# A gated mix of two long convolutions: masked sines on ScalarE, gate sums with the input as the stationary operand, another layout of the gathered kernel, mixing by group

## The chip, the cores and the metric

The kernel runs on one core of a Trainium2 chip. Its engines work side by side, each through its own queue in order: PE (TensorE: matmuls, and the loads of their stationary operands, shown as PEld), DVE (VectorE), ACT (ScalarE), POOL (GpSimd) and SP, which here only issues DMAs. The metric is the device time of one execution in microseconds; lower is better.

## The reference

Inputs are bf16; the sequence has 2048 steps and 448 lanes. From `u` three things are computed and mixed:

```python
g = sigmoid((u * gate_w).sum(-1, keepdims=True))
# a: K[d,l] = Re sum_n C*dt*B * exp(dt*A*l)   (448 lanes, 256 modes, 2048 steps)
a = causal_conv(u, K) + u * Dskip             # by zero-padded FFTs of 4096
# b: kv = (4-tap shift of k) * v
b = u * (causal_conv(kv, ssm_k) + kv * ssm_D)
return g * a + (1 - g) * b
```

## The kernel before

**Layout.** The 128 partitions hold 4 groups of lanes times 32 blocks of time: partition 32 g + a, and on the free axis 64 steps of time and 112 lanes (`uu`, `kt`, `vt`, `ug` are all [128, 64, 112]). The loops go over `H` = 0 to 3, a window of 28 lanes of each group, so 112 lanes at once.

**A convolution** is a transform, a product and an inverse, all by matmuls with matrices of sines that the kernel makes itself. `spread` takes one lane's [128, 64] slice as stationary operand and `Wc` as moving operand, into `zs` (32 frequencies k, 4 groups x 28 lanes). `transform` multiplies each k by `s2_W`. `swapped` makes a copy `zsS` with the real and imaginary halves exchanged, by two DMAs; `products` multiplies `zs` and `zsS` with the other factor. `stage_a` with `R` (`sa_R`) gives `U`, and `stage_b` with `G` (`sb_G`, 64 x 2 matrices of 128 x 128) gives back the time axis. `G` is masked: the columns of group g are non-zero only in the rows of that group. Every matmul stage goes through PSUM (three buffers with the tag "ps"), and is evacuated by ACT (`evac`), or by ACT and DVE in turn (`evac_two`, whose argument i chooses).

**Constants** are made at the start. `stage_b` in the class `Consts` writes phases with DVE, takes their sine with ACT (`sb_v`), and multiplies it with the four columns of the mask on DVE, 16 products in all.

**The kernel K** of convolution a is made by `KGen` in eight blocks of 14 lanes per group. DVE builds powers in `TQ` and `TP` (tiles kg_TQ, kg_TP, with kg_P between), PE sums over modes into `pk`, ACT evacuates to `kg_S`, `gather` arranges the steps by small matmuls into two PSUM tiles that are evacuated to `KT`, and `spread` with `WcK` takes it on. `Tables` makes the exponentials and sines of each pair of blocks in `ET`.

**The gate.** DVE multiplies `uu` with the weights into `ug`, 14 matmuls with a matrix of ones (128 x 128, 512 moving columns) sum eight lanes at a time, DVE reduces, ACT takes a tanh, and DVE makes `gt`, `gb` = g and `og` = 1 - g.

**The end.** Window 3 of convolution a is done in two halves of 14 lanes (`transform_half`, `last`, `stage_a_half`). `mix` multiplies `ug` (result of b) with og, `uu` (by then result of a for windows 0 to 2) with gb, and adds the two for 84 lanes, in eight instructions by halves of the time axis. The last `stage_b` gives four banks of 16 steps; for each DVE multiplies with the gate (`ept`), adds into `ug`, and four DMAs store it, two from SP's queue and two from ACT's.

**Order.** Nothing is issued as the program text runs. `Order` records all 6437 calls, and `issue` replays them in the order of the list `ORDER`, which is written out; each engine keeps that order. The one line that does it is 146, so the profile shows L146 for everything, and groups are told apart by their tiles:

```python
for f, args, kw in self.calls[int(a):int(b or a) + 1]:
    ins = f(*args, **kw)
```

Of the kernel before, what the change touches and what calls it, by code (L numbers as in the profile page):

```python
# [17 lines left out]
P = 128  # L18
# [4 lines left out]
NQG = 4  # L23
# [18 lines left out]
    "681 106 18 113 40 1 270 145 0 114 39 257 274 272 268 275 253 105 109 269 273 255 271 276 256 254 240 104 149 266 "  # L42
    "277 241 267 24 251 3 242 632 672 625 103 108 50 252 634 22 614 244 258 31 38 112 9 604 623 259 111 64 94 42 679 "
    "110 261 10 633 260 46 41 19 278 624 122 61 674 635 49 153 147 30 281 98 282 4 263 246 120 95 2 13 84 45 121 247 "
    "11 154 99 14 155 76 280 16 626 151 47 97 77 96 156 680 21 607 117 20 262 636 25 248 56 608 7 63 15 128 264 17 75 "
    "32 72 37 627 146 55 48 639 23 44 88 150 66 637 29 90 78 249 69 640 118 8 152 83 36 80 629 85 53 107 57 43 628 "
    "101 51 12 119 631 87 62 65 59 630 58 116 74 100 159 35 638 60 52 115 92 265 70 605 79 180 91 6 124 33 27 67 5 26 "
    "71 123 54 82 28 68 102 148 89 659 86 81 125 93 606 34 73 660 144 670 616 667 671 243 668 673 609 245 132 665 661 "
    "250 126 666 662 279 669 663 283 675 129 676 611 677 610 130 157 160 127 181-188 158 131 133-134 170 136 143 135 "
    "220 142 171-178 189 141 161-168 179 200 190 201-208 169 210 304-311 209 294-301 312-320 617 321 230 191-198 "  # L50
    "211-218 199 302-303 615 331-338 219 678 322-329 613 346 339 221-228 612 229 364-379 664 618 231-238 380 330 239 "
    "347-362 621-622 284-291 363 619 381-396 293 397-405 292 1093 620 406 341 1094 434-441 340 1091 416-423 442 1092 "
    "407-414 342 424 343 415 344-345 551 657 561 565 595 658 566 592 560 553 591 443 554-555 550 547 446 466-481 552 "
    "549 548 444 449-464 482 573 769-784 586 465 569 587 500-507 445 508 786-801 785 557 425-432 581 683 641 483-498 "
    "684 642 802 568 596 687 597 572 578 689 582 686 583 598 433 584 688 499 685 1095 562 577 509-516 556 588 563 "
    "690-703 558 589 567 559 590 1109 2471 564 579 593 580 570 594 447 574 571 599 575 527-534 448 643 704 518-525 "
    "137 2516 600 2517 138 601 2477 139 2478 603 602 576 140 1097 1096 2475 2493 535 1098 2494 1099 526 536-543 1105 "
    "705 1100 2472 706 544 1101 644 708 2480 1103 2476 585 707 1106 517 1108 2473 545 653 2474 645 2479 656 646 649 "
    "1111 647 682 651 1107 650 726-741 1113 648 1110 654 1102 655 760-767 652 742-758 1112 1835 768 1114 709-724 546 "
    "759 803-818 725 1115 819 898-905 1104 829-844 906 1117 1120 889-896 845 820-827 1834 828 1122 880-887 897 1836 "  # L60
    "907-914 1837 888 1116 934-941 915 863-878 1838 942 1118 1498-1505 1840 1506 1447-1462 879 952-959 1119 1842 960 "
    "916-923 1124 1463 846-861 1121 1123 924-932 862 1839 1443 1464-1479 933 943-950 1125 1444 1841 2495 1541-1556 "
    "1843-1844 1126 951 1480 2485 1127-1350 2486 1845-1846 2487 2496-2498 1445 2499 2502 2500 1446 2501 1507-1522 "
    "1351-1368 1848 1558-1565 1847 2503 1369 1850 2504 1370-1409 1849 2505 1410 2507 1851 1411-1418 2506 1853 2508 "
    "1852 1419 2482 2509 1566 1420-1427 2481 1523 1854 1618-1625 2483 1855 1524-1539 1856 2518 1428 2484 2491 1626 "
    "2490 1429-1434 1857 1540 1861 961-1024 2510 1859 2512 1557 1858 1481-1496 2492 1672-1679 1863 1830 1435 2520 "
    "1680 1829 1860 1436-1441 1832 1025 1442 1601-1616 1497 1831 1862 2236-2243 1617 1636-1643 2511 2521 2513 1864 "
    "1026-1089 2522 2543 2514 2526 2525 1865-2088 2488 2528 2527 2489 1090 2530 2533 2544 2556 2244 2545 1833 2546 "
    "2515 2547 2519 1644 2548 2529 2523 2531 2549 2524 2550 2539 1663-1670 2538 2089 2559 1645-1652 2558 2542 2554 "
    "1671 3315 2552 2090-2106 2537 1681-1688 1653 2555 1567-1582 2561 1689 2557 2932-2947 1583 2563 1627-1634 2560 "  # L70
    "2569 1635 1654-1661 2107 1584-1599 2562 1662 2571 2564 2108-2147 2535 2182 1600 2565 2181 2148 1699-1762 2566 "
    "2536 2567 2532 2534 2551 2541 2948 2174-2179 2568 2949-2964 1763 2180 1690-1697 2540 2149-2156 2965 3951 2573 "
    "1764-1827 1698 2553 2157 2570 2184 2167-2173 2158-2165 3958 3996 2166 2183 3959 3954-3955 3957 3960 3953 3965 "
    "3956 2245-2260 3314 3952 1828 2572 2296-2303 2261 2279-2294 3966 2574 2304 2202-2217 3997 2295 3316 2185-2200 "
    "2575 2218-2234 3323 2576-2799 3317 2201 3318 2235 3319 3967 3321 3324 3326 3974 3968 2323-2330 3973 2800 3329 "
    "3975 2894-2901 3327 3331 2331 3976 3333 2801-2817 2921-2928 2902 3962 2332-2339 3325 3961 2929 3335 2903-2910 "
    "3328 3337 3963 3330 3682-3697 2911 3964 3977 3332 2818 2305-2312 3978 3338 2340 2819-2858 2313 2912-2919 "
    "3339-3340 2859 3320 2314-2321 2920 2869-2876 3334 2322 2992-3007 3979 3322 2893 2262-2277 3998 3987 3980 3969 "
    "3971 2892 3986 3981 3970 3336 3988 3999 2278 3989 3341 3972 2341-2404 3008 4005 3983 3982 3698 3342 3984 4006 "
    "3343 4022 2931 2983-2990 2966-2981 4020-4021 4019 2991 3344 2982 4008 3345-3568 4001 4014 2930 4009-4010 4016 "  # L80
    "4012 4023 4017 4011 4007 4000 2877 4795 3991-3992 4002 2405 3985 4025 3990 4794 4003 3130-3137 3993 4027 4796 "
    "4004 4026 3139-3146 3994 3569 4797 3995 3043-3050 4036 3138 4798 2878-2883 4039 4038 4028 3051 3716-3723 2884 "
    "4041 2406-2469 3724 4029 3147 4043 4030 4013 3699-3714 2470 3103-3110 2885-2890 4032 3715 3009-3024 4034 3025 "
    "4799 3121-3129 3086-3101 4035 4801 3111-3119 4024 4037 4463-4470 3102 4804 4803 3120 3026-3041 4040 2891 3661 "
    "3052-3067 4806 3042 4042 4045 2860-2867 3662 4018 3069-3084 3068 4031 2868 3166-3173 4471 4047 3588-3627 3085 "
    "4033 3148-3155 4053 3628 3665-3680 4015 3156 3570-3586 4044 5371 4052 3681 3157-3164 4046 3165 3175-3182 4054 "
    "3587 4809 3249-3312 3183 4049 3174 4811 4051 5374 5372 3663 5378-5379 5377 5376 3654-3659 3184-3247 5375 3313 "
# [534 lines left out]
def body(  # L622
# [188 lines left out]
    def block(j):  # L811
# [3 lines left out]
        if KA[H] is None:  # L815
            KA[H] = qt([P, 32, 4 * NC], "zsK")
# [158 lines left out]
```

## Time and profile before

| what | us |
|---|---|
| three runs | 310.83, 310.70, 307.97 (median 310.7) |
| the profiled execution | 308.75 |
| its span, first to last instruction | 307.0 |
| busy in the span: DVE, ACT, PE | 275.5, 250.3, 220.9 |
| table loads on ACT | 15 of 1.28 each |
| mean granted clock of PE | 0.859 of full |

In a line of groups, out<-in are tiles, then come partitions x elements and types, the count, busy time and mean nanoseconds of one instruction, and behind the second bar the idle time in front of them with what ended it. In the answer by stretches the columns are the stretch, its length, busy time (and instructions) of PE, PEld, DVE, ACT and POOL, the granted clock of PE, the share of the DMA engines and GB/s. Lines of the timeline have start, duration, engine, operation and tiles.

### The profile page before, as it was taken

The page shows a single profiled execution, that of the slowest core. Times are in us where ns is not written, and L with a number is a line of the kernel's source. Part 1 is how long each engine was busy: PE and PEld are TensorE (multiplying, and loading weights), DVE is VectorE, ACT ScalarE, POOL GpSimd, SP SyncE. Part 2 cuts the span into 40 slices and gives each one's busy share as a digit, 9 for nine tenths or more (in the row PEclk, how much of TensorE's full clock was granted, in tenths as well). Part 3 has the DMA queues.
Part 4 walks back from the last instruction along what each step waited for, and adds up shares of the span by engine and source line. Part 5 has one row for each costly group of instructions (what it writes and reads, how often), then busy time and mean ns, then how long its engine had stood idle before and what let it go on. Part 6 is the DMA issues. An engine that isn't in the chain of part 4 may idle for free.

```text
span 307.0 us, 11924 instructions
## 1 busy us (share of the span) xinstructions
PE 220.9 (72%) x5287; PEld 192.6 (63%) x5287; DVE 275.5 (90%) x549; ACT 250.3 (82%) x404; POOL 19.1 (6%) x122
## 2 busy tenths in 40 slices
PE   0049973581787688796986598988868989789750
PEld 0013553441777588686976598877867979679740
DVE  8999999969999999999899999798999899972771
ACT  4743589999999499996899999999998997858610
POOL 9101102700000000000000000000000000000000
PEclk9995997768598679997998579979867799999975
DMA  5899999137005003060005002400031000550066
GB/s 110 170 194 167 164 170 253 55 67 113 2 2 122 4 15 49 5 165 4 4 4 121 4 2 46 127 0 6 2 84 42 2 2 4 122 125 5 2 113 129
DMA packets 53380, 21.33 MB, mean 69 GB/s; under 512 B 48720, under 2 KB 51664, under 8 KB 53328
## 3 DMA queue, kind: packets, MB, share of 16 engines
q1 hardware_dynamic: 48768, 19.42, 34.2%
q10 hardware_dynamic: 4560, 1.15, 1.9%
q8 instruction: 41, 0.67, 0.9%
q14 instruction: 11, 0.09, 0.1%
HBM read 10.01 MB, written 3.21 MB: 43 GB/s over the span
## 4 chain that ended last, share of the span: by engine, by line
ACT 39%; PE 26%; DVE 25%; issue 4%; DMA 4%; SPq 0%; DVEq 0%; ACTq 0%
ACT zs L146 14%; ACT ET L146 9%; PE ps_c L146 7%; ACT zsK L146 5%; PE ps_a L146 5%; PE pk L146 5%; ACT U L146 4%; DMA zsS<-zs 4%; PE ps_b L146 3%; PE ps_v L146 3%; PE ps L146 3%; DVE zs L146 2%; DVE zsS L146 2%; DVE kg_P L146 2%; DVE kg_TP L146 2%
## 5 line engine op out<-in xcount | busy, mean ns | idle before, releaser
L146 ACT CAST zs<-ps_c 128x1024 bf16<-128x1024 f32 (+1 forms) x48 | 43.2, 928 | 2.3 <-PE ps_c L146 2.1
L146 DVE TENSOR_TENSOR kg_P<-kg_TQ,ET 128x896 bf16<-128x896 bf16 (+2 forms) x64 | 44.1, 708 | 0.3
L146 ACT CAST zs<-ps 128x896 bf16<-128x896 f32 x48 | 43.5, 930 | 0.8 <-PE ps L146 0.7
L146 PEld LDWEIGHTS <-s_W 128*128 128x128 bf16 x544 | 30.4, 103 | 15.1 <-issue 11.5
L146 PE MATMUL ps_a<-sa_R,zs 128*128 128x128 bf16 x224 | 35.6, 247 | 1.9 <-ACT zs L146 1.3
L146 PE MATMUL pk<-kg_TP,kg_TQ 128*21 128x32 bf16 x1792 | 29.6, 238 | 9.5 <-issue 5.6
L146 PE MATMUL ps_a<-sa_R,zsS 128*128 128x128 bf16 x224 | 34.9, 244 | 1.6 <-DVE zsS L146 1.6
L146 PE MATMUL ps<-zs,s_W 128*128 128x112 bf16 x384 | 28.1, 223 | 9.7 <-ACT zs L146 8.0
L146 PEld LDWEIGHTS <-kg_TQ 128*21 128x21 bf16 x1792 | 27.5, 121 | 11.2 <-issue 10.5
L146 ACT CAST U<-ps_a 128x1024 bf16<-128x1024 f32 (+2 forms) x32 | 30.2, 955 | 3.5 <-PE ps_a L146 3.3
L146 PEld LDWEIGHTS <-zsS 128*128 128x128 bf16 x224 | 31.0, 154 | 3.3 <-DVE zsS L146 1.7
L146 PE MATMUL ps_b<-U,sb_G 128*128 128x28 bf16 x1024 | 28.3, 177 | 5.2 <-ACT U L146 4.9
L146 PEld LDWEIGHTS <-zs 128*128 128x128 bf16 x224 | 30.8, 153 | 1.9 <-DVE zs L146 0.6
L146 PEld LDWEIGHTS <-sb_G 128*128 128x128 bf16 x1024 | 27.5, 97 | 6.4 <-issue 5.6
L146 DVE TENSOR_TENSOR kg_P<-kg_TP,ET 128x1792 bf16<-128x1792 bf16 (+1 forms) x32 | 30.9, 970 | 0.1
L146 DVE TENSOR_TENSOR kg_TQ<-kg_P 128x896 bf16<-128x896 bf16 (+2 forms) x64 | 27.7, 445 | 0.1
L146 PEld LDWEIGHTS <-scratch 128*128 128x128 bf16 x65 | 7.4, 115 | 30.1 <-issue 27.0
L146 PE MATMUL ps_c<-WcK,kg_KT 128*64 128x128 bf16 x224 | 19.0, 294 | 7.9 <-ACT zsK L146 6.6
L146 ACT CAST zsK<-ps_c 128x512 bf16<-128x512 f32 (+2 forms) x28 | 21.6, 780 | 3.2 <-PE ps_c L146 2.9
L146 ACT ACTIVATE ET<-ks_ph 128x448 bf16<-128x448 int16 x40 | 22.7, 599 | 1.2 <-DVE ks_ph L146 1.2
L146 ACT ACT_TABLE_LOAD x15 | 19.2, 1283 | 4.1 <-DMA kt<-in_B_k_dram 3.9
L146 PEld LDWEIGHTS <-kg_KT 128*64 128x64 bf16 x224 | 16.5, 209 | 9.2 <-issue 6.7
(127 smaller groups left out, 468.5 us busy)
## 6 DMA issues: line engine op xcount, KB each, us to landing
zsS<-zs SPq DMA_DIRECT2D x16, 448.0 KB, 5.1
kt<-in_B_k_dram SPq DMA_DIRECT2D x16, 112.0 KB, 3.1
uu<-in_A_u_dram SPq DMA_DIRECT2D x4, 448.0 KB, 8.5
skraw<-in_B_ssm_k_dram SPq DMA_DIRECT2D x16, 112.0 KB, 4.5
vt<-in_B_v_dram SPq DMA_DIRECT2D x4, 448.0 KB, 8.9
xfd<-ks_hold SPq DMA_DIRECT2D x2, 672.0 KB, 4.9
ks_xf<-xfd SPq DMA_DIRECT2D x3, 336.0 KB, 3.3
out_dram<-ug SPq DMA_DIRECT2D x8, 112.0 KB, 3.6
```

The lines of the kernel that those rows point to most:

```text
L146: ins = f(*args, **kw)
```

## The change

Five things, and a new list.

1. The mask of `G` holds the scale of the phase instead of 1/2048, and ACT writes `G` directly: four sines for each of the four quarters, with the mask's column as per-partition scale (outside the group the scale is 0, and so is the sine). The sixteen products and `sb_v` go. The factor 1/2048 is put on `R`, by one DVE instruction.
2. The gate's sums: `gwt` holds the weights, masked by block of time; 112 matmuls take a lane of `uu` (64 columns) as stationary operand and 32 columns of `gwt` as moving operand. The result, 64 x 32, is copied four times side by side, transposed with an fp32 identity, and goes to the tanh. The seven products with DVE and the reduce go.
3. `KT` is [128, 14, 64] for [128, 64, 14]: a lane's 64 columns lie side by side.
4. `mix` goes by window: eleven instructions of 28 lanes. Window 3's product with uu, og and the windows 0 and 1 can stand early; window 2's product with gb and add wait for its result.
5. In block 7 the second evacuation of `gather` and of `spread`, and in `stage_a_half` the second of each half, go to DVE.

The new list holds 6531 calls. It orders all engines' instructions and the DMAs anew, not those of the changed parts alone. Two places matter for what follows: at the start, the sixteen sines stand on ACT among the evacuations of `ps_v` to `kt`, with all of the products that make `kvt` behind each other on DVE; in the tail, PE has both parts of window 2's `stage_b` ahead of the last `stage_a_half`, and DVE has window 2's two mixing instructions ahead of the first `ept`, and the four stores follow each other.

```diff
@@ stage_a (constants)
         nc.scalar.activation(R[:], low16(ph.rearrange("p i b -> p (i b)")), ACT.Sin, scale=PHASE)
+        nc.vector.tensor_scalar(out=R[:], in0=R[:], scalar1=1.0 / 2048, scalar2=None, op0=ALU.mult)
@@ stage_b (constants)
-            v = pool.tile([P, 16, 2, 32], bf16, name="sb_v", tag="kg_P4", bufs=2)
-            nc.scalar.activation(v[:].rearrange("p b r a -> p (b r a)"), low16(ph[:].rearrange("p b r a -> p (b r a)")),
-                                      ACT.Sin, scale=PHASE)
             for g in range(4):
-                nc.vector.tensor_scalar(out=G[:, b0:b0 + 16, :, g, :], in0=v[:], scalar1=mask[:, g:g + 1], scalar2=None, op0=ALU.mult)
+                nc.scalar.activation(G[:, b0:b0 + 16, :, g, :].rearrange("p b r a -> p (b r) a"),
+                                     low16(ph[:].rearrange("p b r a -> p (b r a)")).rearrange("p (c a) -> p c a", a=32), ACT.Sin, scale=mask[:, g:g + 1])
@@ gather
-        KT = self.pool.tile([P, 64, CB], bf16, name="kg_KT")
+        KT = self.pool.tile([P, CB, 64], bf16, name="kg_KT")
...
-                evac(KT[:].rearrange("p (b r) n -> p r b n", r=8)[:, r - 3:r + 1], pt[:, 0:448].rearrange("p (r b n) -> p r b n", r=4, b=8))
+                evac(KT[:].rearrange("p n (b r) -> p n b r", r=8)[:, :, :, r - 3:r + 1], pt[:, 0:448].rearrange("p (r b n) -> p n b r", r=4, b=8), r // 4)
@@ body
-    ones = wp.tile([P, P], bf16, name="ones")
-    V.tensor_scalar(out=ones[:], in0=cons.iota("ones_j", [[0, 4], [1, 32]]), scalar1=a1[:, 0:1], scalar2=None, op0=ALU.is_equal)
+    one = cons.carve(32).bitcast(bf16).rearrange("p (a t) -> p a t", t=2)
+    V.tensor_scalar(out=one.rearrange("p a t -> p (a t)"), in0=cons.iota("one_j", [[1, 32], [0, 2]]), scalar1=a1[:, 0:1], scalar2=None, op0=ALU.is_equal)
+    gwt = qt([P, 32, 112], "gwt")
+    V.tensor_tensor(out=gwt[:].rearrange("p a (n t) -> p a n t", t=2), in0=gw[:].rearrange("p (n t) -> p n t", t=2).unsqueeze(1).to_broadcast([P, 32, 56, 2]),
+                    in1=one.unsqueeze(2).to_broadcast([P, 32, 56, 2]), op=ALU.mult)
@@ block
+        ev = evac_two if j == NBLK - 1 else evac
...
-        cols = lambda c: KT[:, :, c]
+        cols = lambda c: KT[:, c, :]
@@ mix
-        done = 84
...
+        weighed = lambda t, f: V.tensor_tensor(out=paired(t), in0=paired(t), in1=f[:].unsqueeze(2).to_broadcast([P, 64, NC // 2, 2]), op=ALU.mult)
+        for H in range(NQG):
+            o, x = window(ug, 0, 64, H), window(uu, 0, 64, H)
+            if H == NQG - 1:
+                V.tensor_tensor(out=o, in0=o, in1=x, op=ALU.mult)
+            weighed(o, og)
+            if H < NQG - 1:
+                weighed(x, gb)
+                V.tensor_tensor(out=o, in0=o, in1=x, op=ALU.add)
@@ the gate
-    for l in range(0, 112, 16):
-        V.tensor_tensor(out=ug[:, :, l:l + 16], in0=uu[:, :, l:l + 16], in1=gw[:, l:l + 16].unsqueeze(1).to_broadcast([P, 64, 16]), op=ALU.mult)
-    pg = psum.tile([P, 64, 8], f32, name="ps_gate", tag="ps")
-    for l in range(0, 112, 8):
-        nc.tensor.matmul(pg[:], lhsT=ones[:], rhs=ug[:, :, l:l + 8], start=(l == 0), stop=(l == 104))
+    gx = qt([P, 192], "gx", f32)
+    V.tensor_copy(gx[:, 0:64], ident[:, 0:64])
+    pg = psum.tile([P, 512], f32, name="ps_gate", tag="ps")
+    for l in range(112):
+        nc.tensor.matmul(pg[0:64, 0:32], lhsT=uu[:, :, l], rhs=gwt[:, :, l], start=(l == 0), stop=(l == 111))
+    nc.scalar.copy(gx[0:64, 64:192].rearrange("p (g a) -> p g a", g=4), pg[0:64, 0:32].unsqueeze(1).to_broadcast([64, 4, 32]))
+    nc.tensor.transpose(out=pg[:, 128:192], in_=gx[0:64, 64:192], identity=gx[0:64, 0:64])
...
-    V.tensor_reduce(out=gt[:], in_=pg[:], op=ALU.add, axis=mybir.AxisListType.X)
@@ the end
-    stage_a_half(nc, psum, U, R, XA[3], evac, 0)
+    stage_a_half(nc, psum, U, R, XA[3], evac_two, 0)
     last(1)
-    stage_a_half(nc, psum, U, R, XA[3], evac, 1)
+    stage_a_half(nc, psum, U, R, XA[3], evac_two, 1)
```

## The prediction

> **What bounds the kernel now.** I read the page's shares first, then its 40 slices, then busy time by stretches of ten microseconds.
>
> ```profile
> PE 220.9 (72%) x5287; PEld 192.6 (63%) x5287; DVE 275.5 (90%) x549; ACT 250.3 (82%) x404; POOL 19.1 (6%) x122
> ...
> DVE  8999999969999999999899999798999899972771
> ACT  4743589999999499996899999999998997858610
> ```
>
> ```profile
> 0.00:10.00 10.00, 0.00 (x0) 0.00 (x0) 9.08 (x46) 4.43 (x4) 8.37 (x118) 1.00 0.64 124
> 10.00:20.00 10.00, 3.45 (x9) 1.27 (x10) 10.00 (x36) 8.51 (x11) 0.00 (x0) 1.00 0.96 189
> 20.00:30.00 10.00, 6.24 (x19) 2.57 (x19) 10.00 (x6) 2.05 (x3) 0.48 (x1) 0.66 1.36 167
> 30.00:40.00 10.00, 8.91 (x88) 5.54 (x87) 9.38 (x12) 6.07 (x8) 1.63 (x1) 1.00 1.35 164
> 40.00:50.00 10.00, 5.01 (x80) 3.62 (x78) 9.92 (x21) 9.21 (x12) 0.00 (x0) 1.00 1.14 155
> ```
>
> In the second fence the third and fourth busy columns are DVE and ACT. Three stages with three limits: up to 40 us DVE alone is full and ACT idles 19 us; from 40 to about 269 us DVE and ACT are both near full (up to the last product of block 7, which ends at 268.90, DVE idles 13.2 us in all, 0.9 of it at the start, and ACT some 17 after 40); then a tail of 38 us, a chain through PE, evacuations, the last mixes and the stores.
>
> The prices of the parts, from the groups kept apart by shape, and matmuls from the timeline:
>
> ```profile
> L146 DVE TENSOR_SCALAR sb_G<-sb_v,mgB 128x1024 bf16<-128x1024 bf16 x16 | 6.8, 474 | 0.0
> L146 ACT ACTIVATE sb_v<-sb_ph 128x1024 bf16<-128x1024 int16 x4 | 4.2, 1054 | 2.1 <-DVE scratch L146 1.6 <-DVE sb_ph L146 0.4
> L146 DVE TENSOR_TENSOR ug<-uu,gw 128x1024 bf16<-128x1024 bf16 x7 | 4.7, 688 | 0.0
> L146 DVE TENSOR_TENSOR ug<-ug,og 128x3584 bf16<-128x3584 bf16 x2 | 4.0, 2024 | 0.0
> ```
>
> ```profile
> 41.75 0.64 PE L146 MATMUL ps_c<-Wc,skraw 128*64 128x128 bf16 x16 [0.19 <-DVE ks_tC_re L146]
> ```
>
> ```profile
> 264.03 1.87 PE L146 MATMUL ps_c<-WcK,kg_KT 128*64 128x128 bf16 x28 [0.68 <-ACT kg_KT L146]
> ```
>
> **The change, stage by stage.** Neighbours on one engine overlap by some 0.08 us, so sums use start to start.
>
> *Start, DVE.* Removed: 16 products of G at 0.40 = 6.4. Added: the scale of R, 128x256, near the 0.43 of Wc's 128x256 product; below it 0.22 (a 128x128 scale): I take 0.25. So DVE has 6.2 us less. Not all arrives: DVE now meets waits it used to fill. The new list has 13.3 us of DVE work ahead of the first tap product (kvt); the last of the k pieces that it needs is eleventh in SP's queue, and before the eleventh was issued at 8.7 and such pieces landed 2.5 to 4 us later: no wait. The third product needs a piece that is now 22nd (issued 14.2 before): 0 to 1.5 us. The v pieces that the kv products need were landed by some 44 us and stand as far back as before; kv would start at about 46.5 instead of 49.95, and 13 phase instructions (2.4 us) that stood behind kv now stand ahead of it. DVE is 5 to 6 us ahead at 50.
>
> *Start, ACT.* Four sines of 1.05 become 16 (0.97 start to start): +11.6. No row shows a sine with a column as scale and runs of 32 written at a step; the nearest are this one and s_W (2048 elements in runs, 1.91 us, 0.93 ns each against 1.03). I take 0.97; below it 0.9, above twice, 1.95. Added up in the new order, ACT has 37.5 us of work up to the end of the four evacuations of the first k-kernel spread, and cannot start its unbroken run before the second table load, 5.2 us of idle: 42.7, against 45.0 before (26.0 of work). The table loads, 1.28 each, stay 15 by the list. So ACT gains 2.3 where DVE gains 5 to 6.
>
> *Middle, DVE.* Out: seven products for the gate at 0.61 and the reduce 0.6, 4.9. In: gwt, 3584 elements with both inputs repeated, as ug<-ug,og: 2.0, one small mask and one copy 0.3. The mix of 112 lanes in eight halves was 11.4, of which 5.0 stood before 269; now it is eleven instructions of 1792 elements (kv<-vt,kt of that shape: 1.09, 1.0 start to start), nine of them before 269: 9.0 for 5.0, so +4.0. Sum of the middle +1.4. ACT gets one copy, 0.3.
>
> *Middle, PE.* Spreading a block of the gathered kernel reads 64 columns 28 bytes apart: (1.87-0.29)/27 = 59 ns a matmul; skraw, with its columns side by side, (0.64-0.22)/15 = 28 ns at full clock, some 50 at half. 224 matmuls: 4 to 6 us of PE, 0.85 in the last block. The Trainium skill, "TensorE: Matmul & The Clock Gate", section LDWEIGHTS, has the load depend on the number of columns alone, 64/1.2 = 53 ns whatever their step: by it this part would bring nothing; the two rows decide against it. The gate becomes 112 matmuls with uu as stationary operand, 224 bytes a column; the spreads from uu itself run at 59 ns: 6.6 us for 14 at 0.43 (62.67 to 67.98 at half clock), +1.3, where PE was half idle (60 to 80). "Advanced Engine Details and Errata", SBUF Cachelines, speaks against this part: a column per 16-byte line is the slow case, on both operands here; if the moving side paid as much again the gate would be 13 us. The pk matmuls read moving data 448 bytes apart at 15 ns, so I leave it at 6.6. Behind the gate matmuls on PE stand spreads and transforms; ACT has exponentials to do meanwhile. The transpose and its copies add under 2 us to a chain that ends at the gate, and the first mix is far behind it.
>
> At 268.9 then: by DVE -6.2+1.4+0.7 of new waits = -4.1; by ACT -2.3+0.3 = -2.0. Both are near full, so the later rules, and idle time between them stays if the new list feeds them as evenly: -3.0 with shorter PE waits. The list is re-ordered everywhere; I allow 4 us either way.
>
> *Tail.* The chain as it was:
>
> ```profile
> 288.42 1.56 DVE L146 TENSOR_TENSOR ug<-ug,uu 128x2688 bf16<-128x2688 bf16 x1
> 292.12 0.62 DVE L146 TENSOR_TENSOR ept<-ps_b,gt 128x448 bf16<-128x448 f32 x1 [2.14 <-PE ps_b L146]
> 292.77 0.39 DVE L146 TENSOR_TENSOR ug<-ept,ug 128x448 bf16<-128x448 bf16 x1
> ...
> 296.26 1.56 DVE L146 TENSOR_TENSOR uu<-uu,gb 128x2688 bf16<-128x2688 bf16 x1 [0.97 <-ACT uu L146]
> ```
>
> Up to the last evacuation of U (290.27): the last spread -0.85; the second evacuation of KT, spread and two of U go to DVE beside ACT's: about -0.5, -0.5 and -1.0, since PE is busy most of 274 to 289; PE takes 64 matmuls of stage_b (1.7) in, which stood behind: +1.7. Behind it, group 2's two mixes, 2.0, stand ahead of the first ept: first store 3.1 after U, 2.9 before. So the first store moves by -1. The late evacuation of uu (295.32), the mix at 296.26 and its add no longer split the stores: the last add comes 3 us after the first, not 7.4. But the stores take over:
>
> ```profile
> 297.00:300.00 3.00, 0.00 (x0) 0.00 (x0) 3.00 (x4) 0.00 (x0) 0.00 (x0) 0.85 0.92 168
> 300.00:303.00 3.00, 0.00 (x0) 0.00 (x0) 0.52 (x2) 0.00 (x0) 0.00 (x0) 0.50 0.79 151
> ```
>
> 1.84 MB at the 170 to 190 GB/s of 92% to full share take 10 us; with 0.8 ahead and 1 behind, 12 after the first store, for 13.8 before. So -1.8, where DVE alone would give -4. Tail: -2.5.
>
> **Sum.** 308.75 (span 307.0 and 1.75 around it) -3.0 -2.5 = 303.3. The three runs are 307.97 to 310.83, median 310.7; from the median it would be 305.2. I forecast **304**. About 1% is what a measurement of this kernel can tell from no change: under 307.6 is faster, over 313.8 slower.
>
> **Rivals.** (a) *More comes through*, 298: DVE's lead counts (-4), PE's 5 us shorten ACT's waits (-2), and stores run at 230 GB/s, as in single microseconds (-2 more). For it: DVE has the largest share. Against: ACT is as full. Chance 0.15. (b) *ACT takes DVE's place and nothing is left*, 309: from 15 to 43 us ACT has no gap, so its evacuations wait behind sines, PE for banks, DVE for PE; then nothing is won up to 268.9, the tail gives -2.5, and the new order adds 2 to 3 us of stalls in the middle. 0.22. (c) *Slower*, 314: the masked sine itself. At 1.11 start to start ACT's lead of 2.3 is gone; each 0.1 more is 1.6 us on the first evacuations, with nothing to hide it, as ACT stays 95% busy up to 260. At 1.6 it is +10 on the forecast. Against: s_W's strided write is no dearer. 0.15, with all that is slower 0.18. (d) The contiguous KT does nothing (writing runs of four makes the evacuation dearer than 0.57, or loads stay at 59 ns): +1 to +2, inside the range. The forecast itself: 0.45.
>
> Faster 0.60 (forecast and a), same 0.22, slower 0.18. The range 299 to 312 leaves out the far end of (a) and (c); it takes in the 4 us of order either way.
>
> **What will show it.** Sines of G near 1.05 us, 16 of them, ACT without gaps from 15 to 43; the first zs evacuations ending at 42 to 43; DVE busy near 271; spreads from KT near 30 to 50 ns a matmul; gate matmuls 59 ns; block 7's last product at 264 to 268; four adds 1 us apart in the tail, then some 8 us of stores. Wrong if the new order leaves DVE more than 16 us idle before that product, or ACT's sines cost over 1.3.

## The result, and the profile after

The changed kernel takes **319.8 us** (median of four runs, 318.9 to 321.8) against 310.8 for the kernel before in the same comparison: ratio **1.033**, 95% interval 1.024 to 1.042. It is slower; 304 was forecast. The profiled execution took 321.8 us, with a span of 320.0 (before 308.75 and 307.0).

Shares of busy time and the 40 slices of the page:

```profile
PE 228.4 (71%) x5386; PEld 203.8 (64%) x5386; DVE 271.0 (85%) x535; ACT 259.4 (81%) x413; POOL 18.5 (6%) x122
...
DVE  7999996870999999989999989699999999563760
ACT  4599999952999999999799989889999984735600
```

DVE has as little to do as forecast (271), and ACT's start is full. New is a hole in both engines at the ninth and tenth slice, 64 to 80 us; before had 17.0 us of DVE work and 20.0 of ACT work between 60 and 80. By stretches (the columns: PE, weight loads, DVE, ACT, POOL busy, granted clock of PE, DMA share, GB/s):

```profile
0.00:10.00 10.00, 0.00 (x0) 0.00 (x0) 8.02 (x29) 4.31 (x4) 7.30 (x118) 1.00 0.83 138
10.00:20.00 10.00, 0.44 (x1) 0.14 (x2) 9.85 (x44) 7.96 (x11) 0.00 (x0) 1.00 1.10 182
20.00:30.00 10.00, 8.64 (x48) 4.39 (x48) 9.64 (x8) 10.00 (x11) 0.37 (x1) 1.00 1.26 155
30.00:40.00 10.00, 7.44 (x68) 4.50 (x67) 9.60 (x8) 10.00 (x12) 0.00 (x0) 1.00 1.34 166
40.00:50.00 10.00, 5.36 (x87) 4.17 (x85) 9.93 (x30) 9.97 (x16) 0.00 (x0) 0.87 1.22 157
...
60.00:70.00 10.00, 7.39 (x69) 7.39 (x68) 9.88 (x22) 8.38 (x15) 0.00 (x0) 0.50 0.01 3
70.00:80.00 10.00, 10.00 (x98) 9.54 (x99) 0.43 (x2) 2.25 (x6) 0.00 (x0) 0.50 0.00 0
```

From 70 to 80 us PE is the only engine at work. The two new kinds of instruction, from the groups by shape:

```profile
L147 ACT ACTIVATE sb_G<-sb_ph,mgB 128x1024 bf16<-128x1024 int16 x16 | 17.7, 1149 | 0.0
...
L147 PE MATMUL ps_gate<-gwt,uu 128*64 128x32 bf16 x112 | 13.4, 289 | 1.5 <-ACT zs L147 1.5
```

And the hole itself, from the timeline:

```profile
63.86 13.15 PE L147 MATMUL ps_gate<-gwt,uu 128*64 128x32 bf16 x110 [1.52 <-ACT zs L147]
...
77.28 0.26 ACT L147 COPY gx<-ps_gate 64x128 f32<-64x128 f32 x1 [8.88 <-PE ps_gate L147]
...
79.57 0.20 DVE L147 TENSOR_SCALAR gt<-gt 128x64 f32<-128x64 f32 x1 [9.69 <-ACT gt L147]
```

110 gate matmuls in 13.15 us are 120 ns each (118 from start to start). ACT has the copy out of the gate next in its queue and stands 8.9 us before it; DVE has the first operation on gt next and stands 9.7. Spreads and transforms stand behind the gate on PE. The first term's last product ends at 93.2 us (before 83.0). Of these 10 us, 7.5 are still there at block 7's last product (276.4, before 268.9), and at the end of the span it is 13.

The last block's spread and DVE's end:

```profile
274.19 1.71 PE L147 MATMUL ps_c<-WcK,kg_KT 128*64 128x128 bf16 x28 [0.64 <-ACT kg_KT L147]
```

```profile
303.33 1.09 DVE L147 TENSOR_TENSOR uu<-uu,gb 128x1792 bf16<-128x1792 bf16 x1 [1.25 <-ACT uu L147]
304.46 1.09 DVE L147 TENSOR_TENSOR ug<-ug,uu 128x1792 bf16<-128x1792 bf16 x1
305.51 0.62 DVE L147 TENSOR_TENSOR ept<-ps_b,gt 128x448 bf16<-128x448 f32 x1
306.17 0.39 DVE L147 TENSOR_TENSOR ug<-ept,ug 128x448 bf16<-128x448 bf16 x1
...
309.74 0.39 DVE L147 TENSOR_TENSOR ug<-ept,ug 128x448 bf16<-128x448 bf16 x1
```

Four adds about 1.2 us apart, and stores until 320: 13.4 us from the end of the first add (before 13.8).

### The profile page after: what moved, and what is told of

It reads as the page before. It is cut to its first block, busy times and chain, and to the rows that moved or that the text cites. A ratio compares the mean times of both kernels' runs of the same rounds, so it can differ in the third digit from the quotient of the medians.

```text
span 320.0 us, 12122 instructions
## 1 busy us (share of the span) xinstructions
PE 228.4 (71%) x5386; PEld 203.8 (64%) x5386; DVE 271.0 (85%) x535; ACT 259.4 (81%) x413; POOL 18.5 (6%) x122
## 4 chain that ended last, share of the span: by engine, by line
ACT 47%; PE 30%; DVE 7%; DMA 6%; issue 5%; SPq 1%; ACTq 0%; DVEq 0%
ACT zs L147 14%; ACT ET L147 11%; PE ps_a L147 7%; PE ps_b L147 6%; PE ps_c L147 5%; ACT sb_G L147 5%; PE ps_gate L147 4%; ACT U L147 4%; PE ps L147 4%; ACT zsK L147 3%; ACT L147 3%; DMA kt<-in_B_k_dram 3%; PE pk L147 2%; ACT ks_mag L147 2%; DVE kg_P L147 2%
## 5 line engine op out<-in xcount | busy, mean ns | idle before, releaser
L147 PEld LDWEIGHTS <-s_W 128*128 128x128 bf16 x544 | 35.6, 113 | 27.6 <-issue 25.5
L147 PE MATMUL ps<-zs,s_W 128*128 128x112 bf16 x384 | 30.8, 239 | 21.0 <-ACT zs L147 14.4
L147 ACT CAST zs<-ps_c 128x1024 bf16<-128x1024 f32 (+1 forms) x48 | 42.7, 919 | 3.1 <-PE ps_c L147 1.7
L147 ACT CAST zs<-ps 128x896 bf16<-128x896 f32 x48 | 42.7, 930 | 0.4 <-PE ps L147 0.3
L147 PE MATMUL ps_a<-sa_R,zs 128*128 128x128 bf16 x224 | 37.4, 255 | 0.9 <-ACT zs L147 0.9
L147 PE MATMUL ps_a<-sa_R,zsS 128*128 128x128 bf16 x224 | 36.6, 252 | 0.0
L147 ACT CAST U<-ps_a 128x1024 bf16<-128x1024 f32 (+2 forms) x30 | 27.6, 924 | 4.8 <-PE ps_a L147 4.6
L147 PEld LDWEIGHTS <-uu 128*64 128x64 bf16 x336 | 28.7, 213 | 3.2 <-issue 2.3
L147 PEld LDWEIGHTS <-scratch 128*128 128x128 bf16 x65 | 6.6, 103 | 29.4 <-issue 13.5
L147 PE MATMUL ps_v<-kvt,scratch 128*128 128x448 bf16 x64 | 14.5, 377 | 11.0 <-DVE kvt L147 8.5
L147 ACT CAST zsK<-ps_c 128x512 bf16<-128x512 f32 (+2 forms) x27 | 20.6, 766 | 2.1 <-PE ps_c L147 2.1
```

## The experiments

Ratios are against the kernel before, timed on the same chip, with 95% intervals; not all runs were on one chip, so runs are compared with each other by their ratios. 1% is 3.1 us. A `...` in a code cut stands for lines left out.

### The gate

**The gate of before in the changed kernel.** Only the gate's lines change; the order list keeps its places.

```diff
-for l in range(112):
-    nc.tensor.matmul(pg[0:64, 0:32], lhsT=uu[:, :, l], rhs=gwt[:, :, l], ...)
+for l in range(0, 112, 16):
+    V.tensor_tensor(out=ug[:, :, l:l + 16], in0=uu[:, :, l:l + 16], in1=gw[...], op=ALU.mult)
+for l in range(0, 112, 8):
+    nc.tensor.matmul(pg[:], lhsT=ones[:], rhs=ug[:, :, l:l + 8], ...)
...
```

> The changed kernel with the gate of before in it: seven products on DVE right after the last kv product (4.9 us), 14 matmuls with the ones stationary at the place of the 112, the reduction, then the tanh where it stood. Theory A, the 112 gate matmuls are what costs (13.4 us of PE at granted clock 0.50, with 8.9 us of ACT and 9.7 us of DVE waiting behind them): the stretch from 64 to 77 us shrinks to about 6 us, the two waits fall below 2 us, and the time comes to 307 to 312 us. Rival B, the sixteen masked sines have filled ACT from 15 to 60 us and everything after them is late for that reason: the time stays within 2 us of 319.8 us.

Measured: 312.5 us, ratio 1.010 (1.007 to 1.014). Between 60 and 80 us the engines work again:

```profile
60.00:70.00 10.00, 7.12 (x54) 3.87 (x54) 8.25 (x20) 9.38 (x17) 0.00 (x0) 0.64 0.40 92
70.00:80.00 10.00, 6.09 (x85) 5.35 (x86) 9.77 (x25) 10.00 (x23) 0.00 (x0) 0.87 0.01 2
```

The first term's last product is 9.1 us earlier (84.1), and everything behind it up to the end is earlier by 8.3 to 11.7. So the gate costs 7 to 9 us, and the masked sines don't explain the result. (This kernel also has 99 fewer matmuls than the changed one, which shifts the places where PE waits for instructions, see the last of the experiments; the run with halves, below, does not.) The seven products cost nearly nothing here: they fill 3.6 us in which DVE of the changed kernel waits for ACT, from 53 us on.

**The moving operand side by side.** Why 120 ns and not 59? The first thought was the moving operand's step of 224 B.

```diff
-gwt = qt([P, 32, 112], "gwt")
+gwt = qt([P, 112, 32], "gwt")
...
-    nc.tensor.matmul(pg[0:64, 0:32], lhsT=uu[:, :, l], rhs=gwt[:, :, l], ...)
+    nc.tensor.matmul(pg[0:64, 0:32], lhsT=uu[:, :, l], rhs=gwt[:, l, :], ...)
```

> The changed kernel with the gate's moving operand laid out with the 32 columns of one matmul next to each other (gwt as 112 x 32 instead of 32 x 112; one more small copy of gw on DVE). If the step of 224 B of the moving operand makes half of the 120 ns of a gate matmul: 59 to 62 ns a matmul as in the spreads with the same stationary columns, the gate takes 6.6 to 7 us, and the time is 313 to 316 us. If the clock of 0.50 or the short matmul itself makes it: 115 to 120 ns, 13 us, and 319 to 322 us.

Measured: 318.9 us, 1.032 (1.028 to 1.037); 110 matmuls in 13.03 us, 118 ns. The moving operand's step has no part in it.

**What a matmul costs, kind by kind.**

```diff
+for lhs, rhs, halves, places in (...):
+    for l in range(56):
+        h, w = 64 * (l % halves), l % places
+        nc.tensor.matmul(pr[h:h + 64, w, 0:n], lhsT=lhs(l), rhs=rhs(l), ..., tile_position=(0, h))
```

> The changed kernel with nine groups of 56 extra matmuls behind its last one, results unused; they differ in where the stationary columns come from (uu at steps of 224 B, or G with its columns side by side), where the moving ones do (uu at 224 B, 32 of G, 128 of G), whether successive matmuls go to the same half of the array's columns or in turns to both, and whether they accumulate in one place or in two. A1 (load and matmul of the same half are serial): strided stationary, same half 110 to 120 ns, in turns 59 to 65; packed stationary, same half 55 to 65, in turns 28 to 35. A2 (clock): all of a kind alike, and 59 at full clock. A3 (accumulating in the same 32 places has to wait for the one before): two places give 59, one place 117. The time itself says nothing, some 35 us are added.

Measured, start to start within each group, from the instructions' start times in the trace:

```
stationary 64 columns   moving              halves   places   ns
uu, step 224 B          32 of uu, 224 B     same     one      117
uu                      32 of uu, 224 B     in turns one       63
uu                      32 of uu, 224 B     same     two      119
G, side by side         32, side by side    same     one       52
G                       32, side by side    in turns one       28
uu                      128, side by side   same     one      116
uu                      128, side by side   in turns one       62
uu                      32, side by side    same     one      117
uu (first kind again)   32 of uu, 224 B     same     one      118
```

Two windows, the first with 128 moving columns, the second (the table's last line) with 32; the third number from the end is the granted clock:

```profile
328.00:332.00 4.00, 4.00 (x37) 4.00 (x35) 0.00 (x0) 0.00 (x0) 0.00 (x0) 0.72 0.01 4
...
344.00:348.00 4.00, 4.00 (x36) 4.00 (x36) 0.00 (x0) 0.00 (x0) 0.00 (x0) 0.50 0.00 0
```

37 and 36 matmuls in 4 us, at clock 0.72 and 0.50. For stationary columns at a step of 224 B in one half, neither the clock, nor the moving columns' number or step, nor the accumulator matters. Two things do: the step of the stationary columns (52 to 117), and whether successive matmuls go to the same half of the array's columns or in turns to both, which halves either number. So the load of 64 columns is what a matmul costs here: 117 ns at a step of 224 B, 52 side by side (this one at clock 0.50 alone). The 59 and 28 ns of the spreads are half of that, because a spread sends each column once to each half. With 128 moving columns and a load this short the clock does count: spreads with columns side by side run at 28 ns at clock 1.00 and at 52 at 0.50, in the kernel before:

```profile
76.02 2.34 PE L146 MATMUL ps_c<-Wc,skraw 128*64 128x128 bf16 x40 [4.77 <-POOL skraw L146]
```

The Trainium skill says both things: "TensorEngine Tiling (Array Packing)", Key Properties, that tiles load and multiply in parallel, with which the halving agrees (117 to 63); "TensorE: Matmul & The Clock Gate", The mechanism, that loads overlap matmuls in flight only when the row group differs, with which it does not: here all 128 rows are the same and only the columns differ.

**The gate in both halves.** Two accumulators, added by the last matmul.

```diff
 for l in range(112):
-    nc.tensor.matmul(pg[0:64, 0:32], lhsT=uu[:, :, l], rhs=gwt[:, :, l], ...)
+    h = 64 * (l % 2)
+    nc.tensor.matmul(pg[h:h + 64, 0:32], lhsT=uu[:, :, l], rhs=gwt[:, :, l], ..., tile_position=(0, h))
...
```

> The changed kernel with the gate's 112 matmuls in turns in the left and the right 64 columns of the array (two accumulators on partitions 0 to 63 and 64 to 127, added by the last matmul, which takes the place of the transpose). In the spreads the same stationary columns of uu take 59 ns a matmul, and there successive matmuls go to different halves. Theory A1, in the gate the load and the matmul of one half follow each other: now 59 to 65 ns a matmul, the gate takes 7 us instead of 13.2, the waits of ACT and DVE shrink by as much, and the time is 312 to 315 us. Rival A2, the clock of 0.50 (or something else that is the same in both halves) makes the 117 ns: nothing changes, 318 to 321 us.

Measured: 313.2 us, 1.010 (1.007 to 1.014), and the gate is

```profile
63.83 6.81 PE L147 MATMUL ps_gate<-gwt,uu 128*64 128x32 bf16 x111 [1.52 <-ACT zs L147]
```

61 ns a matmul at the same clock of 0.50. ACT's wait falls from 8.9 to 2.4 us, DVE's from 9.7 to 3.3, and the first term's last product comes at 86.9 us for 93.2: the 6.3 us that the gate is shorter, in full. This kernel has one matmul more than the changed one and its stalls for instructions (below) stand at the same places, so they don't explain the gain. That settles the gate. What stays is 1%, where the forecast had 2% less than before.

### The masked sines

**The sines alone, in the kernel before.** Four masked sines stand at the place of each plain one.

```diff
-nc.scalar.activation(v[...], low16(ph[...]), ACT.Sin, scale=PHASE)
 for g in range(4):
-    nc.vector.tensor_scalar(out=G[:, b0:b0 + 16, :, g, :], in0=v[:], scalar1=mask[:, g:g + 1], ...)
+    nc.scalar.activation(G[:, b0:b0 + 16, :, g, :]..., low16(ph[...])..., ACT.Sin, scale=mask[:, g:g + 1])
...
```

> The kernel before with the masked sines alone: four masked sines at the place of each of the four sines, the sixteen products gone from DVE, R scaled. Theory A (the gate is what costs): the sines cost ACT 11 to 13 us of the start, where DVE is relieved of 6; the time is 309 to 314 us. Rival B (the sines are what costs): 318 to 323 us, like the changed kernel.

Measured: 318.5 us, 1.030 (1.024 to 1.036), in the rival's range, but not for the rival's reason. Eight of the sixteen now stand in ACT's queue ahead of the copy of the taps, for which all kvt products wait:

```profile
DVE kvt L146 <- ACT scratch L146: 6.7, 1, 6.7
```

In the changed kernel's list that copy comes first and DVE has no such wait. This run prices the place, not the sines.

**The sines taken back, in the kernel with the old gate.** Four plain sines and sixteen masked copies on DVE, as before; the order of the rest stays.

```diff
+nc.scalar.activation(v[...], low16(ph[...]), ACT.Sin, scale=PHASE)
 for g in range(4):
-    nc.scalar.activation(G[:, b0:b0 + 16, :, g, :]..., low16(ph[...])..., ACT.Sin, scale=mask[:, g:g + 1])
+    nc.vector.tensor_scalar(out=G[:, b0:b0 + 16, :, g, :], in0=v[:], scalar1=mask[:, g:g + 1], ...)
...
```

> e1_old_gate (the changed kernel with the gate of before) with G written as before too: four plain sines at the places of the first masked sine of each block, sixteen products on DVE among the kvt products, R unscaled. If the masked sines on ACT (17.7 us between 15 and 41 us) set the pace of the start: ACT gains 13 us there, and the time falls by 3 to 6 us from 312.5, to 306 to 309. If DVE sets it (no gap on it from 10 to 60 us in that kernel): the products add 5 to 6 us there, and the time is 315 to 319 us.

Measured: 317.3 us, 1.023 (1.017 to 1.029), 4 us slower than with the masked sines. DVE sets the start there:

```profile
20.00:30.00 10.00, 7.59 (x40) 3.68 (x39) 9.97 (x14) 4.22 (x5) 0.44 (x1) 1.00 1.33 171
30.00:40.00 10.00, 7.54 (x56) 4.39 (x56) 10.00 (x13) 3.68 (x5) 0.00 (x0) 1.00 1.35 164
```

DVE is full and ACT (fourth pair) has 12 us free; the last kv product is done at 58.6 us instead of 53.3, and that lasts to the end. In their own list the masked sines gain 4 us.

### The layout of kg_KT, the mixing and the late evacuations

**The layout alone, in the kernel before.**

```diff
-KT = self.pool.tile([P, 64, CB], bf16, name="kg_KT")
+KT = self.pool.tile([P, CB, 64], bf16, name="kg_KT")
...
-cols = lambda c: KT[:, :, c]
+cols = lambda c: KT[:, c, :]
```

> The kernel before with nothing changed but the layout of kg_KT (one column's 64 values next to each other), same order list. If the layout is worth what the prediction put on it: spread matmuls of kg_KT at 28 to 35 ns a start instead of 59, about 0.7 us of PE less in each of eight blocks, and 308 to 310 us. If PE is not what the blocks wait for: 310 to 311 us, as before. If the eviction pays for the writing in steps of 16 B: over 312 us.

Measured: 309.7 us, 0.997 (0.993 to 1.002). At most a small gain, though the last block's spread takes 0.97 us instead of 1.87, at clock 1.00 and 28 ns a matmul:

```profile
279.94 0.97 PE L147 MATMUL ps_c<-WcK,kg_KT 128*64 128x128 bf16 x28
```

**The late second evacuations on DVE, in the kernel before.**

```diff
-stage_a_half(nc, psum, U, R, XA[3], evac, 0)
+stage_a_half(nc, psum, U, R, XA[3], evac_two, 0)
...
```

> The kernel before with the late second evacuations on DVE as the changed kernel has them (one gather, one spread, two of stage_a_half), same order list. The prediction's step: ACT's last evacuations no longer stand behind one another, 1 to 2.5 us less, 308 to 309.5 us. Rival, PE or DVE is what those places wait for: 310 to 311 us; or worse, because DVE takes its instructions in order and now waits for PE before the mixing: 311 to 313 us.

Measured: 309.4 us, 0.999 (0.995 to 1.003): nothing that can be told from zero.

**The end of before behind the front of the changed kernel with the old gate.** The mixing and the late evacuations are those of before, and so is the order of what the list issues last.

```diff
-ev = evac_two if j == NBLK - 1 else evac
-KT = kg.gather(j, S, ev)
+KT = kg.gather(j, S, evac)
...
-for H in range(NQG): ...
+for t, n, f in ((uu, done, gb), (ug, 112, og)): ...
```

> e1_old_gate with the end of before: mixing in halves of the rows as before, all late evacuations on ACT, and the calls that start after 258 us in the order that the kernel before has them in. In e1_old_gate block 7's evacuation is 1.2 us later than in the kernel before, but the first of the four last adds 4.6 us later (297.8 against 293.2), because the mixing of a whole window waits for both halves of the rows and the first store for it. If that is so: first add at 293 to 294 us, end 3 to 4 us earlier, 308 to 310 us. If it is the lower clock of the end (0.63 between 260 and 280 us against 1.00): 311 to 313 us, as e1.

Measured: 312.6 us, 1.009 (1.005 to 1.013), no better than without it. Its first add ends at 298.4, in step with a block 6 that is late (its kg_S at 261.6 against 258.3): calls that the changed list had done by 258 us and those that it had not are not the same as before, and the splice made block 6 wait for them. It does not say what the end is worth.

**The mixing moved, in the kernel before (with the contiguous kg_KT).** Windows 0 and 1 go into DVE's idle time at 277 us, window 2 is done in the two halves of the rows.

```diff
-for t, n, f in ((uu, done, gb), (ug, 112, og)): ...
+for H, b0, n in ((0, 0, 64), (1, 0, 64), (2, 0, 32), (2, 32, 32)):
+    x, o = window(uu, b0, n, H), window(ug, b0, n, H)
+    weighed(x, gb, b0, n)
+    V.tensor_tensor(out=o, in0=o, in1=x, op=ALU.add)
```

> The kernel before with the contiguous kg_KT (alone 309.7 us) and the mixing by window, but otherwise than in the changed kernel: windows 0 and 1 in DVE's idle 5.5 us at 277 us (four operations of 1.09), window 2 in the same two halves of the rows as before (four operations of about 0.55 where four of 1.55 stood). If the last two mixing operations at 296 and 298 us were on the path to the last add: last add 2 us earlier, 307 to 309 us. If the stores bound the end from the first add on (13 us in each run so far): the first add is not moved, since it waits for PE, and the time stays at 309.5 to 310.5 us.

Measured: **307.7 us, 0.993 (0.989 to 0.996)**: 0.7% faster than the kernel before. How much of it is the mixing is not shown: the interval overlaps that of the layout alone (0.993 to 1.002). DVE's end there:

```profile
274.23 1.08 DVE L147 TENSOR_TENSOR uu<-uu,gb 128x1792 bf16<-128x1792 bf16 x1
...
295.37 0.63 DVE L147 TENSOR_TENSOR uu<-uu,gb 128x896 bf16<-128x896 bf16 x1 [0.88 <-ACT uu L147]
...
296.22 0.62 DVE L147 TENSOR_TENSOR ug<-ug,uu 128x896 bf16<-128x896 bf16 x1
...
297.40 0.39 DVE L147 TENSOR_TENSOR ug<-ept,ug 128x448 bf16<-128x448 bf16 x1
```

The last add ends at 297.8 instead of 300.6, and the first one, still waiting for PE, at 292.4 instead of 293.2. The span ends 12.9 us after the first add, where before needed 13.8. The 0.8 us of the first add need not come from the mixing: in this execution block 7's pk matmuls run without the stall of 1.0 us that they have in before's (below).

**The same with the late evacuations on DVE too.**

> e10_mix (the kernel before with contiguous kg_KT and the mixing moved, 307.7 us) with the late second evacuations on DVE besides (alone 309.35 against 309.9). If the two gains add: 306.5 to 307.5 us. If the four operations that now fill DVE's gap at 277 us and the evacuations are in one another's way: 308 to 309.5 us.

Measured: 309.4 us, 0.997 (0.992 to 1.001): no sign that they add; the interval overlaps that of the mixing alone.

### The place of the instruction pieces

Without the slow gate the changed kernel reaches block 7's last product at 267.7 (before 268.9), but its evacuation of kg_S is 1.2 us late and the last of U 5.4. In between PE stands still in the middle of the pk matmuls, with no wait that the profile shows:

```profile
273.63 1.58 PE L147 MATMUL pk<-kg_TP,kg_TQ 128*21 128x32 bf16 x91 [3.52 <-issue]
```

The trace records packets of 16 KB on an instruction queue, 41 of them, for 5,287 matmuls with as many loads: some 128 matmuls a packet (a piece; where one ends and the next begins is a border). One began to arrive at 270.9, took 1.4 us, and PE went on at 273.6. If that is the cause, extra matmuls far ahead move the border. Spare ones were put into PE's wait at 55 us:

```diff
+for i in range(64):
+    h = 64 * (i % 2)
+    nc.tensor.matmul(spare[h:h + 64, 0:32], lhsT=Wc[:, 0:64], rhs=Wc[:, 64:96], ..., tile_position=(0, h))
```

> e1_old_gate with 64 spare matmuls (results unused) on PE in its wait of 5.7 us at 55 us; they change nothing but the place of every later PE instruction in the stream that PE fetches in pieces of 16 KB. In e1_old_gate such a piece began to arrive at 270.9 us, behind the swap transfers, and PE stood 3.5 us in the middle of block 7's pk matmuls with nothing to wait for but instructions; then the granted clock was 0.50 for 12 us. If the place of the pieces is what the end loses by: the stall at 270 us moves or shrinks below 1.5 us, and the time is 308.5 to 311 us. If not (312.5 us measured for e1_old_gate): 312 to 313.5 us.

Measured: 309.8 us, 1.001 (0.998 to 1.004), clear of the 1.010 (1.007 to 1.014) without spare matmuls.

> As e11_shift64, with 96 spare matmuls. If pieces of 16 KB hold 256 instructions, that is 128 matmuls with their loads, this moves every border by three quarters of a piece. Theory of the pieces: stalls at other places than in e1_old_gate and e11_shift64, and a time that differs from both by 1 us or more; rival: all three within 1 us.

Measured: 310.9 us, 1.003 (1.000 to 1.007): the median is 1 us or more from both others, but the interval overlaps that with 64 and touches that with none.

> e1_old_gate with 128 spare matmuls in the same place, a whole piece of instructions by the count of the stalls (91 matmuls of block 7 were left behind the stall with none, 27 with 64, 59 with 96). Theory of the pieces: the borders lie where they lay in e1_old_gate, 91 matmuls left again and 312 to 313.5 us. Rival, that any spare matmul helps (a warmer clock, say): 309 to 311 us, like the 64 and the 96.

Measured: 312.3 us, 1.007 (1.002 to 1.012). The stall in block 7 with 64, 96 and 128 spare matmuls:

```profile
272.92 0.60 PE L147 MATMUL pk<-kg_TP,kg_TQ 128*21 128x32 bf16 x27 [2.88 <-issue]
```

```profile
274.30 1.08 PE L147 MATMUL pk<-kg_TP,kg_TQ 128*21 128x32 bf16 x59 [2.69 <-issue]
```

```profile
273.71 1.57 PE L147 MATMUL pk<-kg_TP,kg_TQ 128*21 128x32 bf16 x91 [2.23 <-issue]
```

91 matmuls are left with none, 27 with 64 (91 + 64 - 128), 59 with 96, and 91 again with 128. The border is where the count puts it, exactly. With 128 the other stalls are back as well: the last seven before block 7's leave 66, 136, 8, 2, 27, 130 and 2 matmuls of their blocks, the same numbers as with none. By the medians 128 spare matmuls give most of the time back that 64 had taken away. The stall itself did not shrink below 1.5 us as expected. By 231 us the kernel with 64 is 1.7 us ahead of the one with none (which stands still for 1.3, 1.8 and 1.6 us at 202, 219 and 223 us, the one with 64 for 0.9 and 1.7), and the rest of the gain comes behind the stall in block 7. The intervals of 64 and of 128 overlap a little (1.004 against 1.002), so that the place of the stalls follows the count is shown, and that the time follows it with 128 is likely and no more.

The place isn't all. The profiled execution with 128 took 309.7 us, 2.6 below that kernel's median, with the borders where they lie with none. Up to 265 us it is 1.6 us behind the one with none, and at the end 2.9 ahead: its stall in block 7 is 2.2 us for 3.5, and behind it the clock is back to 1.00 by 280 us (third number from the end), where without spare matmuls it is 0.50 up to 283 (lines under "Tail" below):

```profile
275.00:280.00 5.00, 3.72 (x116) 2.98 (x106) 2.91 (x6) 2.62 (x5) 0.00 (x0) 0.79 0.02 3
280.00:285.00 5.00, 5.00 (x108) 4.91 (x103) 2.35 (x4) 4.34 (x5) 0.00 (x0) 1.00 0.01 3
```

**The same in the kernel before**, in its wait at 71 us:

> The kernel before with 64 spare matmuls in PE's wait of 4.8 us at 71 us. If the place of the pieces is a price that any version pays by chance: the stall of 1.0 us before the last 105 matmuls of block 7 moves (105 + 64 = 169, or 41 left), and the time moves by 1 to 3 us, more likely up, to 311 to 313 us. If only the changed list is open to it: 309.5 to 310.5 us.

Measured: 314.1 us, **1.013 (1.005 to 1.022)**. Before, block 7 lost 1.0 us with 105 matmuls left, and block 5 1.3 us with 73 left:

```profile
229.45 1.30 PE L146 MATMUL pk<-kg_TP,kg_TQ 128*21 128x32 bf16 x73 [1.31 <-issue]
...
272.19 1.80 PE L146 MATMUL pk<-kg_TP,kg_TQ 128*21 128x32 bf16 x105 [0.96 <-issue]
```

With 64 spare matmuls:

```profile
233.07 0.34 PE L147 MATMUL pk<-kg_TP,kg_TQ 128*21 128x32 bf16 x9 [3.20 <-issue]
...
278.32 0.84 PE L147 MATMUL pk<-kg_TP,kg_TQ 128*21 128x32 bf16 x41 [2.63 <-issue]
```

9 is 73 + 64 - 128 and 41 is 105 + 64 - 128. The spare matmuls themselves delay nothing: at 100 us this execution is 1.4 us ahead of before's. It then falls back, mainly in four steps at 152, 230, 260 and 274 us, each behind such a stall, and ends 5.7 behind: 7.1 us lost, where its stalls inside the pk matmuls add up to 12.6 us and before's to 5.6. So the kernel before, as it stands, is spared some 4 us by the place of its pieces. No run with 128 spare matmuls was made in it; that it is their place and not their presence rests on this sum of two traces.

**Both cures in the changed kernel**, halves and 64 spare matmuls:

> The changed kernel with the gate's matmuls in turns in both halves of the array's columns (e5_halves, 313.2 us) and 64 spare matmuls in PE's wait at 55 us, which move the borders of the instruction pieces by half a piece. Theory: the serial loads (7 us) and the place of the pieces (2.7 us, e1_old_gate against e11_shift64) add up and are independent: 309.5 to 311.5 us. Rival: the spare matmuls helped e1_old_gate by something else: 312.5 to 314 us.

Measured: 311.7 us, 1.005 (1.001 to 1.009), 1.5 us off where 2.7 were expected, just outside the range, and not clear of noise (1.007 to 1.014 with the halves alone).

## Why the prediction was wrong, by its steps

Put together: the change stands at +3.3%. The gate is 2.3 of it (1.033 to 1.010, by the halves and by the old gate alike). The place of the instruction pieces is up to 0.9 with the old gate (1.010 to 1.001); with the halves it is 0.5, within the noise. The rest of the change nets to between nothing and a small loss, where the forecast had -2%. The sign of being wrong that the prediction named is there: DVE idles 25.2 us before block 7's last product, over the 16 that were allowed.

- **Gate, the step that failed.** "The spreads from uu itself run at 59 ns: 6.6 us." The row was right and the reading wrong: 59 ns was the mean of two halves that load side by side, 117 the price of one. The gate was to take 6.6 us; it took 13.4. And the sum at 268.9 goes by DVE (-4.1) and ACT (-2.0) alone and has no term for the gate's matmuls at all: their extra length on PE was put at nothing, because PE was half idle there. The doubt that stood beside it (13 us, if the moving side paid as much again) had the size, put it on the wrong operand, and was left out of the range on the strength of the pk matmuls' 15 ns, which also go in turns to different columns. The clock of 0.50, an obvious suspect, has no part: 61 ns at 0.50 once the halves alternate, and 116 at 0.72 to 1.00 in one half.
- **"ACT has exponentials to do meanwhile"** failed with it. They stood behind the copy out of the gate in ACT's queue, and kg's products behind the operations on gt in DVE's. So the gate's length on PE became waits of 8.9 and 9.7 us on the two engines that set the pace, where the sum had taken it as hidden. The transpose and its copies were named; who is queued behind them was not.
- **Start, DVE.** kv was to start at 46.5 and starts at 49.2. DVE idles 3.0 us up to 50 us where before idles 1.6; no run accounts for the remaining difference. The sign was right: the products on DVE again cost 4 us (e7).
- **Start, ACT.** The last evacuation of the first spread ends at 45.6 (forecast 42.7, before 45.0), so ACT's lead is gone. The sine was put at 0.97 us start to start and is 1.05 (from each sine's start to the next instruction's; the 17.7 us of busy time for 16 counts their overlapping ends): 1.3 us for 16, short of the 1.11 at which rival (c) had the lead gone. ACT's idle time ahead of its unbroken run is 7.8 us where the sum had 5.2: 2.5 more. Mechanism right, both terms mis-sized. Rival (c) ended on the right side by another mechanism: in this list the sines gain.
- **Middle.** -3.0 at block 7's last product: with the slow gate it is +7.5; with the old gate -1.2, with 64 spare matmuls on top -3.0 (265.9). That last agreement is luck: -3.0 was the sum's -2.0 and 1.0 more for which the prediction showed no row. The last spread from kg_KT takes 1.71 us instead of 1.87, forecast 0.85 less, got 0.16. Its price was right at full clock (0.97 us in the kernel before with the layout alone); in the changed kernel the clock is 0.50 there, and it takes 52 ns a matmul. And the layout alone is worth 0.3%, not to be told from zero.
- **Tail, the second step that failed.** Forecast -2.5 (its own terms, -1 up to the first store and -1.8 in the stores, add up to -2.8). From block 7's last product to the end of the span it was 38.1 us; it is 43.6, 43.1 with the old gate, 41.8 with 64 spare matmuls. The late evacuations on DVE bring nothing alone (e13). A stall for instructions was not thought of, and neither was the clock: in the kernel with the old gate PE runs at

```profile
265.00:268.00 3.00, 3.00 (x45) 2.83 (x46) 2.66 (x4) 2.92 (x5) 0.00 (x0) 0.50 0.30 65
...
274.00:277.00 3.00, 2.52 (x116) 2.11 (x104) 0.99 (x2) 1.43 (x3) 0.00 (x0) 0.50 0.02 5
277.00:280.00 3.00, 2.34 (x44) 1.71 (x44) 1.70 (x3) 0.91 (x3) 0.00 (x0) 0.50 0.03 5
280.00:283.00 3.00, 2.67 (x38) 2.50 (x39) 0.92 (x1) 1.44 (x2) 0.00 (x0) 0.50 0.00 0
```

  where the kernel before has 1.00 in each of these stretches. The stall of 3.5 us stands before the second of them; that it brings the clock down was not tried by itself, and the first line, ahead of it, is at 0.50 too. How the 3.7 us by which this tail stays longer with 64 spare matmuls divide between clock, stalls and order is open. That the order alone is not the price shows in the execution with 128: the same list, a stall of 2.2 us, the clock at 1.00 again by 280, and a tail of 38.7 us.
- **Stores.** The adds come nearly as close together as forecast (the last 3.6 us after the first, forecast 3), but from the first add to the end it is 13.4 us, forecast 12, before 13.8: of 1.8 us to be gained, 0.4 came.

## What to carry to other kernels

A matmul's spacing in a trace is a price only with its neighbours: with short moving operands ask whether successive loads go to the same columns of the array, and let them alternate (117 to 63 ns, 52 to 28). At a lower clock the moving columns can take over as the price: 28 ns at 1.00 became 52 at 0.50 with 128 of them. Before pricing a new chain at its own length, list what stands behind each of its links in every engine's queue; here a side result that nobody needs for 78 us (gt at 79.6, the first product with og at 157.9) held up three engines. In a kernel within 1% of its neighbours, shift the instruction stream by half a piece and look again before believing a ranking.

## What the runs showed of the hardware that was not expected

- The load of 64 stationary columns takes 52 ns side by side (at clock 0.50) and 117 at a step of 224 B, this one at granted clocks of 0.50 and of 0.72 to 1.00 alike. In turns to the two halves of the array's columns the spacing halves, so the two halves load at the same time.
- PE gets its instructions in pieces of 128 matmuls with their loads. In pk runs at 15 to 28 ns a matmul it waits between nothing and 3.5 us at a border, and the place of the border follows the count exactly: in all 18 traces every stall of over 0.2 us inside these runs stands 85 to 92 matmuls past a multiple of 128. The Trainium skill, "Runtime: NRT & Kernel Launch", Instruction fetch mechanics, has the size (blocks of 256 instructions, with which the count agrees) and calls the crossing mostly hidden; in these rows it is not. What a border costs varies from run to run: in the kernel before the one in block 7 cost 1.0 us, with the layout changed alone 0.3, and with the mixing moved nothing. Why one costs 1.0 us and another 3.5 was not tried: in the long case the swap transfers had the DMA engines busy (DMA share 0.97 from 268 to 271 us), which is argued, not shown.
- 64 spare matmuls changed a time by -0.9% in the one kernel and by +1.3% in the other.
